# Third pair of row buffers, a narrower memory update, and a new order table in a two-layer attention and Fourier kernel

## The chip, the cores and the metric

The kernel runs on one core of a Trainium2 chip. The metric is the device time of one execution in microseconds (us), taken as the median of several runs. Engines are named as the profile names them: PE multiplies matrices (PEld is its weight load), DVE, ACT and POOL are the vector, scalar and GpSimd engines, and SP issues all DMAs here.

## The reference, cut to what matters

Four sublayers follow each other on x of 2048 rows and 512 columns: attention, Fourier mixing, attention, Fourier mixing. Attention is split into four segments of 512 rows and 32 heads of 16 columns:

```python
for s in range(N):                       # N = 4 segments of L = 512 rows
    logits = einsum("bhqd,bhkd->bhqk", qs, ks) * scale + mask
    a_dot = einsum("bhqk,bhkd->bhqd", softmax(logits), vs)
    pq = phi(qs)                         # phi(t) = t + 1 if t > 0 else exp(t)
    a_mem = einsum("bhld,bhde->bhle", pq, M) / (einsum("bhld,bhd->bhl", pq, z) + 1e-6)
    o = g * a_mem + (1 - g) * a_dot      # outs.append(o)
    M = M + einsum("bhld,bhle->bhde", phi(ks), vs)      # the memory update
    z = z + phi(ks).sum over l
# x = x + A(layernorm(x)); x = x + real(DFT_seq(DFT_hidden(layernorm(x)))), twice
```

The mask hides keys behind the query.

## The kernel before

The heads are worked on in four *groups* of eight heads (`HG = 8`, as two halves `a` of `NP = 4` pairs `p`). A group in a segment of a layer has the number `i` from 0 to 31; `q = i // 4` is its segment over both layers. Its steps are small Python generators ("streams", `s_...`, one for each kind of work, and "tasks", `t_...`, one for each tile). A planner (`Plan`) keeps a modelled clock for each engine. In a loop it takes the step that could start first, less the advance that `LEAN` gives to this kind of step on this engine, and records its instructions. So the code is written out once, in one fixed order for each engine; on the chip, each engine runs its list in that order and waits on semaphores where data is late. `yield need(...)` is a point at which another step may come between.

The path of a group at the start of the program:

- `t_ln` normalizes a tile of 128 rows of x: statistics on DVE (`bst`, `mv`), the power and two small operations on POOL (`rs`), the scaled copy on ACT, its split into two 16-bit halves `hl`. In the first segment (`direct`) PE transposes it with `identh`, and the result goes to the x tile `g` (`xt`). Projections (`s_p`) wait for all four x tiles of the segment.
- `s_w` finds the largest weight (`absmax`, rows named `amax` and `vm`), makes power-of-two scales (`gmax`, `scl`, `inv`, `fac`) and splits the weights (`split`, `share`) that were staged in rows of the result tile `y`. `t_big` later reads `wo` and `wd` into `y`, `s_wo` finds their largest elements (`pmax`) and splits them; its end is the key `WO`, for which the output projection and the Fourier part wait.
- `t_split` turns q and k into halves, stores them to a scratch `d`, and reads them back in rows `qst` and `kst`. There are `NR = 2` pairs of these row buffers; group `i` may write pair `i % 2` only when the scores of group `i - 2` are through (`ST`).
- `s_x` (X) forms the scores `b<-kst,qst` to find each row's largest one. DVE reads them from PSUM and writes `junk` and `mx`; PE transposes `mx` with `identf`, and `mhl` goes into rows of `qst` by DMA. `s_st` (ST) forms them again, transposed (`b<-qst,kst`); ACT takes the exponential, POOL selects. Two rows of ones per half in `kst` (`KR`) are written by `t_ones`.
- `s_av` (AV) multiplies with `vt`: `b<-w,vt`, in which `vt` is the weight operand, 32 columns wide, and four pairs stand side by side in the array. `s_mem` updates the memory: `b<-vt,w`, with `vt` the moving operand; the result is masked with `bd` and added to `macc`. `s_m` merges to `ot`, and `s_o` projects with `b<-wo,w`.

The tile `vt` holds, for each row and pair, 16 columns of one head's v, 16 ones and 16 columns of the other's:

```python
vt = [const.tile([128, TT, NP, 3, 16], F32, name=f"vt{i}") for i in range(NR)]
```

The Fourier part (`b<-wd,w`, then `b<-w,w`) follows, and fills PE wherever attention leaves room. `t_warm` puts idle multiplications (`b<-onesb`) where the planner expects PE to idle, so that PE's clock stays up. Profile rows carry one line number, that of the recording helper (L272), so rows are told apart by tile names.

Of the kernel before, what the change touches and what calls it, by code (L numbers as in the profile page):

```python
# [19 lines left out]
TT = L // 128  # L20
# [11 lines left out]
TICK = 10240 / 3  # L32
LEAN = dict(s_stT=150.0, s_memV=40.0, s_wV=80.0, s_rY=150.0, t_mergeA=40.0, s_xA=150.0, t_abA=40.0, t_mergeY=-150.0, s_mV=40.0, t_cV=-40.0, s_cA=-80.0, s_oY=40.0, t_cY=80.0, t_lnG=80.0, t_splitV=-40.0, t_phiA=150.0, s_kV=-300.0, t_mergeV=150.0, s_cT=80.0, s_avT=80.0, s_wA=-150.0, t_resV=-150.0, t_selG=40.0, s_lnY=-150.0, t_rowsY=300.0, t_ktY=-80.0)
APART = dict(pj=(1, 4), av=(1, 2), dft=(0, 2), sx=(2, 4), st=(2, 4), ss=(0, 4))
# [7 lines left out]
PRIO = {}  # L42
PHM, EARLYLN, FEW = 5, 1, 0
WARM, IDLE, SPARE = 4200, 500.0, 300.0
DEEP = 1500.0
# [4 lines left out]
class Plan:  # L50
# [31 lines left out]
    def key(self, a):  # L82
        f = self.fine.get(a.tensor.name)
        return (a.tensor.name, a.offset // f) if f else a.tensor.name

# [69 lines left out]
    def op(self, eng, name, args, kw):  # L155
# [19 lines left out]
        elif eng == "A":  # L175
            c = n / 1.2 + (52 if src else 93) + (93 if any(a.free_size() == 1 for a in ins) else 0)
        elif eng == "V":
            c = 68 + n / 0.96
            if name == "reciprocal":
                c = 68 + n * 6.25  # L180
            elif name == "scalar_tensor_tensor" and out[0].dtype == F32:
                c += 60
            elif name == "tensor_copy" and out[0].dtype == F16:
                c = 68 + n / 1.92
            elif name == "tensor_scalar" and out[0].dtype == F32:
                c = 68 + n / (0.87 if src else 1.32)
        elif eng == "G":
            c = 127 + n * 0.915 if name == "affine_select" else 96 + n * 2.1
            if name == "tensor_tensor" and kw.get("op") == OP.pow:
                c = 300 + n * 165  # L190
# [88 lines left out]
def body(ctx: ExitStack, tc: tile.TileContext, x, wq, wk, wv, wo, beta, wd, cs, out):  # L279
# [66 lines left out]
    cmask = const.tile([128, 512], BF16, name="cmask")  # L346
    bd = const.tile([128, 2, 4, 32], F32, name="bd")
    gt = const.tile([128, 2, NG, 2], F32, name="gt")
# [64 lines left out]
    def share(o, src, s):  # L413
        yield need("A", src, s)
        A.activation(o[:, 0], src, AF.Copy, scale=s)
        A.activation(src, src, AF.Copy, scale=s)
        yield need("VG", o, src)
        tt(o[:, 1], src, o[:, 0], OP.subtract)

    def flat(t):  # L420
# [104 lines left out]
    def t_ones():  # L525
# [7 lines left out]
        pl.close(c8)  # L533
        for i in range(NR):
            for a in range(2):
                yield need("Y", d8, mode="b")
                Y.dma_start(kst[i][64 * a + 48:64 * a + 50].rearrange("r p n -> r (p n)"), d8, est=(415, 341, 472))
        done.add("KR")

    def s_k():  # L540
# [12 lines left out]
        for j in range(NR):  # L553
            V.memset(vt[j][:, :, :, 1, :], 1.0)
        done.add("VI")
        yield need("V")
        bits(rp, 3, 1.0)
        bits(ra, 64, 1.0 / 64)
        cj = sb("en", F32, (128, 2, 4, 32))
        G.iota(cj, pattern=[[0, 2], [1, 4], [0, 32]], base=0, channel_multiplier=0,  # L560
# [24 lines left out]
    def t_ln(src, xi, dst, key, direct=False):  # L585
        st = rg("bst", 2, F32, (128, 6))
        V.bn_stats(st, src)
        mv = rg("mv", 6, F32, (128, 4))
        V.bn_aggr(mv[:, 0:2], st)
        yield need("G", mv)  # L590
        rs = rg("rs", 6, F32, (128, 1))
        G.tensor_scalar(mv[:, 2:3], mv[:, 1:2], 1e-5, 2.0 ** -20, op0=OP.add, op1=OP.mult)
        G.tensor_tensor(rs, mv[:, 2:3], mhalf, op=OP.pow)
        G.tensor_scalar(mv[:, 3:4], mv[:, 0:1], rs, -1.0, op0=OP.mult, op1=OP.mult)
        yield need("A", src, mv, rs, tag="hl")
        hl = sb("hl", F16, (128, 2, 512))
        A.activation(xi, src, AF.Identity, bias=mv[:, 3:4], scale=rs)
        if direct and pl.free["V"] < pl.free["A"]:
            yield need("V", xi)
            V.tensor_copy(hl[:, 0], xi)  # L600
        else:
            A.activation(hl[:, 0], xi, AF.Copy)
        yield need("VG", xi, hl)
        tt(hl[:, 1], xi, hl[:, 0], OP.subtract)
        pl.close(xi)
        if direct:
# [6 lines left out]
            yield need("VA", p)  # L613
            if pl.free["A"] <= pl.free["V"]:
                A.activation(dst, p, AF.Copy)
            else:
                V.tensor_copy(dst, p)
# [33 lines left out]
    def t_merge(e, o, gi, g, n, key):  # L651
# [7 lines left out]
        rc = rg("rc", 4, F32, (128, 2, 16))  # L659
        xa = x[:, 0]  # L660

        def view(off, *dims):
            return bass.AP(xa.tensor, xa.offset + off, [list(xa.ap[0])] + [list(d) for d in dims])

        yield need("V", x)
        d = view(16, (496, 2), (32, 16))
        if not gi:
            V.tensor_scalar(rc, d, 1e-6, None, op0=OP.add)
            d = rc
        V.reciprocal(rc, d)  # L670
# [3 lines left out]
        for a in range(2):  # L674
            c = slice(16 * a, 16 * a + 16)
            tt(n.rearrange("p (b r) -> p b r", r=32)[:, :, c], view(528 * a, (32, 16), (1, 16)),
               rc[:, a].unsqueeze(2).to_broadcast([128, 16, 16]), OP.mult)
# [3 lines left out]
    def t_split(p, key, f, kphi):  # L681
# [24 lines left out]
        dst = (qst if order else kst)[i % NR]  # L706
        for a in range(2):
# [52 lines left out]
    def t_v(p, i):  # L760
        yield need("A", p)
        A.activation(vt[i % NR].rearrange("p t j e d -> p (t j) e d")[:, :, 0:3:2, :],
                     p.rearrange("p t (j e d) -> p (t j) e d", j=NP, e=2), AF.Copy, scale=2.0 ** -24)
        pl.close(p)
        done.add(("v", i))
# [72 lines left out]
    def s_mem():  # L838
        for i in range(NGRP):
# [14 lines left out]
            if s < NSEG - 1:  # L854
                yield gate(("phk", i), ("v", i), "GM")
                phk, v = phs["phk", i], vt[i % NR]
                yield need("T", phk, v, tag="pj")
                mp = ps("pj", F32, (128, NP, 48))
                for t in range(TT):
                    T.matmul(mp, phk[:, 128 * t:128 * t + 128], v[:, t], start=(t == 0), stop=(t == TT - 1))  # L860
                    yield need("T")
                pl.close(phk)
                yield need("V", mp, tag="mu" if s else ())
                mu = macc[:, g] if s == 0 else sb("mu", F32, (128, 2, 4, 32))
                for a in range(2):
                    V.tensor_tensor(mu[:, a], mp[:, :, 16 * a:16 * a + 32], bd[:, a], op=OP.mult)
                pl.close(mp)
# [16 lines left out]
    def t_max(sp, mx, a, p0, w, t, left):  # L884
        n = 128 * (t + 1)
        for p in range(p0, p0 + w):
            o = (p - p0) * n
            yield need("V", sp)
            junk = rg("junk", 2, BF16)
            V.tensor_tensor_reduce(junk[:, :n], sp[:, o:o + n], cmask[:, 512 - n:], 1.0, -3e38,  # L890
# [4 lines left out]
    def s_x():  # L895
        for i in range(NGRP):
            yield gate(("dq", i), ("dk", i), "CM")
            qs, ks = qst[i % NR], kst[i % NR]
            mx = rg("mx", 2, F32, (128, 2, NP, TT))
# [46 lines left out]
    def s_st():  # L946
        for i in range(NGRP):
            yield gate(("X", i), "KR")
            qs, ks = qst[i % NR], kst[i % NR]
            kt = scores("t")  # L950
# [142 lines left out]
    def t_c(i, raw, sc, cc):  # L1093
        A.activation(cc[:, 0], raw, AF.Copy, scale=sc)
        A.activation(raw, raw, AF.Copy, scale=sc)
        yield need("VG", cc, raw)
# [7 lines left out]
    def s_c():  # L1104
        k = u = 0
        while u < nunit:
# [17 lines left out]
            pl.close(pm)  # L1124
            gi = gv.bitcast(I32)
            V.tensor_scalar(gi, gi, 0x7F800000, None, op0=OP.bitwise_and)
            V.tensor_scalar(csc[:, :m].bitcast(I32), gi, -1.0, float(268 << 23), op0=OP.mult, op1=OP.add)
            V.tensor_scalar(fyu[:, u:u + m], gv, f_y, None, op0=OP.mult)
# [87 lines left out]
    def t_warm(at):  # L1216
        at -= SPARE
        if "CM" not in done or at - pl.free["T"] < IDLE or pl.lately(at) >= WARM:
            return
# [108 lines left out]
```

## Time and profile before

| what | value |
|---|---|
| median of 3 runs | 1696.49 us (1695.97 to 1700.98) |
| the profiled execution, its own time | 1699.92 us |
| its span, first to last instruction | 1698.2 us |
| mean granted clock of PE | 0.989 |
| busy share PE, DVE, ACT, POOL | 98, 61, 51, 48 % |

An engine's "busy" is the time in which at least one of its instructions was under way. Matmuls are pipelined, so their means (380 ns for 512 columns) are longer than the pace at which they follow each other. A row of the groups reads: engine, operation, out<-in, shapes, count, then busy us and mean ns of one, then the idle time before them and who ended it. In the timeline a row gives start, length, and how many equal instructions in a row it stands for. PE writes two instructions for one multiplication of 32-bit operands, so the 96 of the memory update are 192 rows.

### The profile page before, as it was taken

To read this page: it belongs to the slowest core of one execution; us is meant where nothing else is said; L and a number is where in the kernel's file an instruction comes from. 1 tells how busy PE (TensorE), PEld (TensorE's weight loads), DVE (VectorE), ACT (ScalarE), POOL (GpSimd) and SP (SyncE) were. 2 spreads that over 40 slices of the span, in tenths; PEclk is the share of its full clock that TensorE was granted. 3 is DMA by queue.
4 is the path that set the end of the run, shared out by engine and by line. 5 is a ranking of instruction groups with operands and counts; after the bars stand their busy time and mean duration, and the time that the engine had idled before them with its cause. 6 is when DMAs were issued, how large, how long until landed. Compare 5 with 4: busy or idle time off the path is not lost.

```text
span 1698.2 us, 32247 instructions
## 1 busy us (share of the span) xinstructions
PE 1662.3 (98%) x11145; PEld 734.7 (43%) x11145; DVE 1036.8 (61%) x3262; ACT 872.3 (51%) x1480; POOL 810.3 (48%) x1445
## 2 busy tenths in 40 slices
PE   8889999999999999999999999999999999999999
PEld 4344344444444344444544444443444444444444
DVE  8784865778677786635768558546575765433221
ACT  5487577755656666535376754655455325312000
POOL 4376556575565556634255644635454415322000
PEclk9789999999999999999999999999999999999999
DMA  7546545655357432525746663543435322131423
GB/s 182 147 116 178 128 132 159 172 142 152 94 148 208 126 119 84 189 56 196 193 148 187 182 179 90 132 116 98 140 91 149 105 85 76 57 125 38 143 70 123
DMA packets 208629, 222.92 MB, mean 131 GB/s; under 512 B 104520, under 2 KB 127048, under 8 KB 208464
## 3 DMA queue, kind: packets, MB, share of 16 engines
q1 hardware_dynamic: 208464, 220.85, 45.8%
q8 instruction: 88, 1.44, 0.4%
q14 instruction: 77, 0.63, 0.1%
HBM read 137.40 MB, written 61.87 MB: 117 GB/s over the span
## 4 chain that ended last, share of the span: by engine, by line
PE 77%; DVE 9%; ACT 5%; issue 4%; DMA 3%; POOL 2%; SPq 1%; ACTq 0%; DVEq 0%; POOLq 0%
PE b L272 77%; ACT w L272 4%; DVE junk L272 4%; SPq L272 1%; DVE w L272 1%; POOL w L272 1%; DMA w<-w 1%; DMA w<-x 1%; DVE m L272 1%; DVE mx L272 1%; DVE y L272 1%; DVE bst L272 0%; DVE cam L272 0%; DMA w<-in_cs_dram 0%; DVE pmax L272 0%
## 5 line engine op out<-in xcount | busy, mean ns | idle before, releaser
L272 PEld LDWEIGHTS <-w 128*128 128x128 f16 x5056 | 467.8, 98 | 612.8 <-issue 101.1
L272 PE MATMUL b<-w,w 128*128 128x512 f16 x3072 | 708.5, 380 | 1.7 <-DVE mx L272 0.8
L272 ACT ACTIVATE w<-b,fac 128x512 f32<-128x512 f32 (+1 forms) x728 | 419.2, 655 | 176.3 <-PE b L272 175.8
L272 DVE CUSTOM_DVE_ANT_0 junk<-b,cmask 128x128 bf16<-128x128 f32 (+3 forms) x1024 | 436.3, 483 | 71.6 <-PE b L272 71.1
L272 POOL TENSOR_TENSOR w<-w,w 128x512 f16<-128x512 f32 (+1 forms) x294 | 347.5, 1187 | 247.1 <-ACT w L272 223.6
L272 POOL TENSOR_SCALAR_AFFINE_SELECT w<-w 128x128 f32<-128x128 f32 (+2 forms) x704 | 237.0, 350 | 202.7 <-ACT w L272 194.1
L272 DVE SCALAR_TENSOR_TENSOR y<-b,fyu,y 128x512 f32<-128x512 f32 x200 | 148.9, 745 | 235.6 <-PE b L272 235.2
L272 ACT ACTIVATE w<-w,csc 128x512 f16<-128x512 f32 (+1 forms) x256 | 180.1, 720 | 41.5 <-DVE csc L272 32.8
L272 PE MATMUL b<-g,w 128*128 128x512 f16 x768 | 183.1, 383 | 3.2 <-DMA g<-w 0.8
L272 PE MATMUL b<-wd,w 128*128 128x512 f16 x768 | 176.8, 379 | 0.1
L272 PE MATMUL b<-w,vt 128*32 128x512 f32 (+3 forms) x2048 | 172.4, 449 | 1.9 <-POOL w L272 1.1
L272 ACT ACTIVATE w<-b 128x512 f16<-128x512 f32 x128 | 75.9, 596 | 189.4 <-PE b L272 179.3
L272 DVE SCALAR_TENSOR_TENSOR w<-b,w 128x512 f16<-128x512 f32 x128 | 87.6, 687 | 120.3 <-ACT w L272 118.7
L272 ACT ACTIVATE w<-w 128x512 f16<-128x512 f32 (+1 forms) x137 | 86.5, 632 | 90.1 <-DVE w L272 87.9
L272 PE MATMUL b<-kst,qst 48*128 48x128 f16 (+3 forms) x1024 | 117.5, 304 | 6.3 <-DVE mx L272 3.2
L272 PE MATMUL b<-qst,kst 50*128 50x512 f16 (+3 forms) x1024 | 115.8, 302 | 5.5 <-DVE mx L272 2.2
L272 PE MATMUL b<-w,g 128*128 128x128 f16 x1536 | 96.3, 221 | 0.0
L272 PEld LDWEIGHTS <-g 128*128 128x128 f16 x1536 | 89.6, 99 | 12.7 <-issue 7.8
L272 DVE STREAM_TRANSPOSE m<-b 128x512 f32<-128x512 f32 x112 | 75.6, 698 | 31.1 <-PE b L272 30.7
L272 PEld LDWEIGHTS b<-w,vt 128*32 128x32 f32 x2048 | 54.8, 110 | 87.7 <-issue 48.2
L272 PE MATMUL b<-wo,w 128*128 128x512 f16 x384 | 89.1, 379 | 0.0
L272 PEld LDWEIGHTS <-kst 50*128 50x128 f16 x1024 | 37.3, 94 | 111.7 <-issue 105.2
(105 smaller groups left out, 1019.3 us busy)
## 6 DMA issues: line engine op xcount, KB each, us to landing
w<-in_cs_dram SPq DMA_DIRECT2D x128, 256.0 KB, 3.5
cc<-w SPq DMA_DIRECT2D x128, 256.0 KB, 3.2
w<-cc SPq DMA_DIRECT2D x128, 256.0 KB, 3.1
w<-w SPq DMA_DIRECT2D x96, 256.0 KB, 3.5
d<-w SPq DMA_DIRECT2D x128, 128.0 KB, 2.5
w<-in_x_dram SPq DMA_DIRECT2D x32, 256.0 KB, 3.6
qst<-d SPq DMA_DIRECT2D x64, 128.0 KB, 2.7
kst<-d SPq DMA_DIRECT2D x64, 128.0 KB, 3.3
```

The costliest lines, as they stand in the source:

```text
L272: r = f(*args, **kw)
```

## The change

1. A third pair of row buffers lies in rows 8 to 11 of the result tile `y`, where the value weights were staged. It serves group 2 alone, once all value weights are split. Groups 3 and on use pairs 0 and 1 in turn (`ring`) and wait for the group named in `prior`: group 3 for ST of group 0 (before: of group 1), group 4 for ST of group 1 (before: of group 2), and from group 5 on as before.
2. `vt` is `[128, TT, 32, HG]`: 16 rows of v columns, then 16 of ones, the eight heads innermost. The update reads the first 17 of the 32 (136 columns, before 192); AV takes 32 columns that lie 8 elements apart (before: side by side). The mask is applied in two pieces of the same number of elements, and `bd` is 16 bits wide. The value weights are permuted on the host to fit.
3. In the first segment the small operations of the norms run on DVE, except the power, and the split of the x tile always on DVE.
4. More `yield need(...)` stand between instructions of one tile. The making of `bd` waits for the first scales.
5. Some costs of the planner and some entries of `LEAN` are new, and warming may start before the causal mask is made.

```diff
-LEAN = dict(..., t_abA=40.0, ..., s_oY=40.0, ..., s_cT=80.0, ...)
+LEAN = dict(..., t_abA=150.0, ..., s_cT=150.0, ..., s_ldY=300.0, t_lnA=80.0, t_lnY=-150.0)
...
+    kst.append(y[:, 8:10, :].bitcast(F16).rearrange("p a (b n) -> p (a b) n", n=512))
+    qst.append(y[:, 10:12, :].bitcast(F16).rearrange("p a (b n) -> p (a b) n", n=512))
+    ring = [0, 1, 2] + [(i - 3) % 2 for i in range(3, NGRP)]
+    prior = [None] * 3 + [0, 1] + list(range(3, NGRP - 2))
-    vt = [const.tile([128, TT, NP, 3, 16], F32, name=f"vt{i}") for i in range(NR)]
+    vt = [const.tile([128, TT, 32, HG], F32, name=f"vt{i}") for i in range(NR)]
...
+        if direct and STARTV:
+            yield need("V", mv)
+            V.tensor_scalar(mv[:, 2:3], mv[:, 1:2], 1e-5, 2.0 ** -20, op0=OP.add, op1=OP.mult)
+            yield need("G", mv)
+            G.tensor_tensor(rs, mv[:, 2:3], mhalf, op=OP.pow)
+            yield need("V", mv, rs)
+            V.tensor_scalar(mv[:, 3:4], mv[:, 0:1], rs, -1.0, op0=OP.mult, op1=OP.mult)
...
-        if i >= NR:
-            yield gate(("ST", i - NR))
+        if i == NR:
+            yield gate(*[("W", 2, g) for g in range(NG)])
+        elif i > NR:
+            yield gate(("ST", prior[i]))
...
-                mp = ps("pj", F32, (128, NP, 48))
+                mp = ps("pj", F32, (128, 17, HG))
-                    T.matmul(mp, phk[:, 128 * t:128 * t + 128], v[:, t], start=(t == 0), stop=(t == TT - 1))
+                    T.matmul(mp, phk[:, 128 * t:128 * t + 128], v[:, t, :17], start=(t == 0), stop=(t == TT - 1))
...
-                                 v[:, t, p].rearrange("k e d -> k (e d)")[:, 16 * a:16 * a + 32], tiles[p][1],
+                                 v[:, t, :, NP * a + p], tiles[p][1],
```

How this moves instructions is seen at two places. The first is DVE at the start, up to the copy of the fourth x tile. Before, the statistics of all four tiles stand together ahead of the weights' scales (the rows begin behind the statistics of the first two tiles; `w_85` to `w_91` are the four tiles of x, `w_319` and `w_329` their halves):

```order
L272 BN_STATS bst<-w_89 128x6
L272 BN_AGGR mv<-bst 128x2
L272 BN_STATS bst<-w_91 128x6
L272 BN_AGGR mv<-bst 128x2
L272 CAST w_319<-w_85 128x512
L272 CAST w_329<-w_87 128x512
L272 TENSOR_REDUCE amax<-y 128x1 x2
L272 TENSOR_SCALAR gmax<-b_365 128x2
```

Now the last part of the fourth tile (`w_91`, its halves `w_450`) stands among the scales of the last weights:

```order
L279 CAST w_450<-w_91 128x512
L279 TENSOR_SCALAR gmax<-b_471 128x2
L279 TENSOR_SCALAR gmax<-gmax 128x2
L279 TENSOR_SCALAR scl<-gmax 128x2
L279 TENSOR_SCALAR inv<-gmax 128x2
L279 TENSOR_SCALAR fac<-inv 128x1 x4
L279 TENSOR_REDUCE amax<-y 128x1 x2
L279 TENSOR_TENSOR w_450<-w_91,w_450 128x512
```

Eight small scale instructions behind these rows comes DVE's copy of the fourth tile to the x tile `g`. From the first statistics to it DVE now has 76 instructions. Before, its one copy to `g` was the 18th, and the other three tiles' copies were ACT's.

The second place is SP's queue between the scores X of groups 1 and 2. Before, the row maxima `mhl` of group 1 go out first, then the stores `d` of groups 2 and 3, and the rows of group 2 (into pair 0, `qst_106`) after them:

```order
L272 DMA qst_107<-mhl 1x16x128 x4
L272 DMA d<-w_810 64x2x512 x2
L272 DMA d<-w_1209 64x2x512 x2
L272 DMA_TRANSPOSE w_1239<-w_1209 128x8x128
L272 DMA w_1261<-in_x_dram 128x512
L272 DMA d<-w_1241 64x2x512 x2
L272 DMA d<-w_1268 64x2x512 x2
L272 DMA qst_106<-d 32x2048
```

Now the rows of group 2 go into `y` right behind the row maxima of group 1, and those of group 3 into pair 0 behind them:

```order
L279 DMA d<-w_834 64x2x512 x2
L279 DMA d<-w_1196 64x2x512 x2
L279 DMA d<-w_1252 64x2x512 x2
L279 DMA qst_107<-mhl 1x16x128 x4
L279 DMA y<-d 32x2048
L279 DMA y<-d 16x2048
L279 DMA y<-d 32x2048
L279 DMA y<-d 16x2048 x2
L279 DMA y<-d 32x2048
L279 DMA y<-d 16x2048
L279 DMA y<-d 32x2048
L279 DMA qst_106<-d 32x2048
```

The rows of group 2 no longer wait for the scores of group 0, but they still stand behind `mhl` of group 1.

More of the change, by code (lines that the diff above doesn't have):

```diff
@@ L418, in share, with view @@
         tt(o[:, 1], src, o[:, 0], OP.subtract)
+    def view(t, off, *dims):
+        return bass.AP(t.tensor, t.offset + off, [list(t.ap[0])] + [list(d) for d in dims])
     def flat(t):
@@ L659, in t_merge @@
         rc = rg("rc", 4, F32, (128, 2, 16))
[L660 to L663 removed]
         yield need("V", x)
[L666 removed]
+        d = view(x, 16, (512, 2), (32, 16))
         if not gi:
             V.tensor_scalar(rc, d, 1e-6, None, op0=OP.add)
+            if YM:
+                yield need("V", rc)
             d = rc
@@ L701, in t_split @@
             spawn(t_kt(hl, kphi))
-        if i >= NR:
-            yield gate(("ST", i - NR))
+        if i == NR:
+            yield gate(*[("W", 2, g) for g in range(NG)])
+        elif i > NR:
+            yield gate(("ST", prior[i]))
         yield need("Y", d)
         order = key[0] == "dq"
-        dst = (qst if order else kst)[i % NR]
+        dst = (qst if order else kst)[ring[i]]
         for a in range(2):
@@ L897, in s_x @@
             yield gate(("dq", i), ("dk", i), "CM")
-            qs, ks = qst[i % NR], kst[i % NR]
+            qs, ks = qst[ring[i]], kst[ring[i]]
             mx = rg("mx", 2, F32, (128, 2, NP, TT))
@@ L947, in s_st @@
         for i in range(NGRP):
-            yield gate(("X", i), "KR")
-            qs, ks = qst[i % NR], kst[i % NR]
+            yield gate(("X", i), ("KR", ring[i]))
+            qs, ks = qst[ring[i]], kst[ring[i]]
             kt = scores("t")
@@ L1217, in t_warm @@
         at -= SPARE
-        if "CM" not in done or at - pl.free["T"] < IDLE or pl.lately(at) >= WARM:
+        if at - pl.free["T"] < IDLE or pl.lately(at) >= WARM:
             return
```

74 lines of the change are left out of this document (53 added, 21 removed).

## The prediction, as put on record

> **What bounds the kernel now.** The page comes first: is one engine the bound, and where is it not?
>
> ```profile
> span 1698.2 us, 32247 instructions
> PE 1662.3 (98%) x11145; PEld 734.7 (43%) x11145; DVE 1036.8 (61%) x3262; ACT 872.3 (51%) x1480; POOL 810.3 (48%) x1445
> PE   8889999999999999999999999999999999999999
> PEclk9789999999999999999999999999999999999999
> PE 77%; DVE 9%; ACT 5%; issue 4%; DMA 3%; POOL 2%; SPq 1%; ACTq 0%; DVEq 0%; POOLq 0%
> ```
>
> PE is busy in all slices but the first three or four, and carries 77% of the chain that ended last. So work that is taken from PE behind the start comes off the end, and in the start it is the other engines that decide. The second view is the table of stretches, cut at the events that the timeline shows:
>
> ```profile
> core 0: us, PE busy (x) PEld busy (x) DVE busy (x) ACT busy (x) POOL busy (x), PEclk, DMA share, GB/s
> 0.00:17.00 17.00, 11.34 (x62) 5.11 (x63) 14.10 (x40) 9.35 (x11) 10.07 (x25) 1.00 0.96 247
> 34.00:70.00 36.00, 30.71 (x156) 10.23 (x154) 34.36 (x144) 15.08 (x25) 10.42 (x18) 0.83 0.60 177
> 70.00:91.00 21.00, 20.65 (x175) 10.10 (x174) 8.88 (x30) 14.73 (x27) 12.78 (x25) 0.89 0.62 129
> 91.00:132.00 41.00, 35.55 (x258) 14.68 (x255) 33.59 (x146) 33.98 (x61) 30.15 (x59) 0.79 0.36 96
> 132.00:172.00 40.00, 38.80 (x352) 18.00 (x349) 20.68 (x69) 29.77 (x52) 27.65 (x50) 1.00 0.65 189
> 213.00:1698.00 1485.00, 1469.24 (x9796) 650.20 (x9796) 875.02 (x2675) 733.17 (x1244) 689.09 (x1226) 1.00 0.45 129
> ```
>
> Up to 172 us PE does few instructions per us (156 in 36 us, against 9796 in 1485), partly at a reduced clock (0.79 to 0.89). DVE fills 34 to 70 (34.36 of 36 us), where X of groups 0 and 1 runs, and is nearly idle from 70 to 91. The third view is PE's timeline, for the dates:
>
> ```profile
> 16.88 1.46 PE L272 MATMUL b<-g,w 128*128 128x512 f16 x6 [0.68 <-ACT g L272]
> 18.31 4.04 PE L272 MATMUL b<-g,w 128*128 128x512 f16 x18
> 34.39 0.51 PE L272 MATMUL b<-kst,qst 48*128 48x128 f16 x10
> 69.74 0.39 PE L272 MATMUL b<-identf,mx 128*32 128x128 f32 x1 [1.56 <-DVE mx L272]
> 90.67 0.42 PE L272 MATMUL b<-kst,qst 48*128 48x128 f16 x8
> 131.24 0.27 PE L272 MATMUL b<-identf,mx 128*32 128x128 f32 x1 [0.94 <-ACT w L272]
> 171.61 0.60 PE L272 MATMUL b<-wo,w 128*128 128x512 f16 x2
> ```
>
> The first projections, q and k of group 0, run from 16.88 to 22.35; X of groups 0 and 1 from 34.39 to 69.74 (`identf` is its end); X of group 2 starts at 90.67, and that of group 3 ends at 131.24; the first output projection, from which PE has enough to do, is at 171.61. The hole from 69.74 to 90.67 is the wait for a free pair of row buffers.
>
> **The memory update.** 96 multiplications stand as 192 instructions:
>
> ```profile
> L272 PE MATMUL b<-vt,w 128*128 128x192 f32 x192 | 38.6, 338 | 1.4 <-ACT vt L272 1.2 <-POOL w L272 0.2
> L272 PE MATMUL b<-vt,w x192: 326/326/430, 79.6 to 1260.2; 128*128 128x192 f32 x192
> 79.55 1.57 PE L272 MATMUL b<-vt,w 128*128 128x192 f32 x8
> 82.16 0.92 PE L272 MATMUL b<-vt,w 128*128 128x192 f32 x4
> ```
>
> Four more instructions in a row cost 1.57 - 0.92 = 0.65 us, so the pace is 162.5 ns for 192 columns, 0.846 ns a column. With 136 it is 115 ns if only the columns count: 47 ns saved. What could hold it up is the weight load of 128 columns that lies beside each. The first of a run, whose load has no cover, takes 430 ns against 326, so a load costs 104 ns: just under 115. I take the full 47 ns; the other bound is nothing saved, if a load of 32-bit weights needs more than its 104 ns beside a running matmul. In both orders 20 of the 96 stand ahead of the first output projection, where PE waits anyway; the other 76 are 152 instructions x 47 ns = **-7.1 us** (bounds -7.1 and 0). DVE's mask has as many elements as before, now with a step between them in PSUM; DVE idles for 610 of 1485 us behind 213 and covers it; without that cover it would be 96 pieces with, at most, 0.2 us more each.
>
> **The weight operand of AV**, with a step of 8 elements. Its loads stand beside each other and beside a running matmul:
>
> ```profile
> L272 PEld LDWEIGHTS b<-w,vt 128*32 128x32 f32 x2048 | 54.8, 110 | 87.7 <-issue 48.2 <-POOL w L272 23.4 <-DVE mx L272 3.0
> 81.05 0.85 PE L272 MATMUL b<-w,vt 128*32 128x384 f32 x8
> 81.84 0.39 PE L272 MATMUL b<-qst,kst 50*128 50x256 f16 x4
> ```
>
> At 0.846 ns a column, four side by side, a load of 110 ns lies beside matmuls of 108 ns (128 columns) to 433 ns (512); only the first load behind another kind of work lies open, about 120 times by the order. Of its 110 ns the reading of 32 columns is some 26, a quarter of the 104 of 128 columns. No row shows a stepped load. Bounds: 0 (the same elements; nothing can be gained), and the whole 110 ns once more each time, 13 us. I take 0: most of a load is not reading.
>
> The Trainium skill ("Advanced Engine Details and Errata", SBUF Cachelines) speaks against the change: a line is 16 bytes, full speed needs at least two hits on each, and here neighbours are 32 bytes apart. By that rule, as an estimate at half speed, reading takes 26 ns more at each open load: 3.1 us, and 1691 for the whole. No run here shows it yet; the mechanism is in the third rival.
>
> **Changes of PE's kind of work.** From AV to scores above, 81.84 - 81.05 = 0.79 us, of which 8 x 384 columns, four side by side at 0.846 ns, are 0.65: 0.14 us a change. Behind the first Fourier product the order has 726 such changes before and 749 now: 23 x 0.14 = **+3.2 us**.
>
> **The start.** The 76 instructions that DVE now has ahead of the fourth x tile, by these rows:
>
> ```profile
> 4.24 0.68 DVE L272 BATCH_NORM_STATS2 bst<-w 128x6 f32<-128x512 f32 x1
> 8.60 0.45 DVE L272 CAST w<-w 128x512 f16<-128x512 f32 x1 [0.51 <-ACT w L272]
> 14.28 0.69 DVE L272 COPY g<-b 128x1024 f16<-128x1024 f16 x1 [0.21 <-PE b L272]
> 14.89 1.63 DVE L272 SCALAR_TENSOR_TENSOR w<-y,scl,w 128x512 f16<-128x512 f32 x2
> 19.30 0.17 DVE L272 TENSOR_SCALAR scl<-gmax 128x2 int32<-128x2 int32 x1
> 19.57 0.40 DVE L272 TENSOR_SCALAR fac<-inv 128x1 f32<-128x1 f32 x4
> 19.89 2.46 DVE L272 TENSOR_REDUCE vm<-y 128x1 f32<-128x512 f32 x4
> 25.16 0.68 DVE L272 SCALAR_TENSOR_TENSOR w<-b,w 128x512 f16<-128x512 f32 x1
> L272 DVE TENSOR_TENSOR wd<-y,wd 128x512 f16<-128x512 f32 x1 | 0.9, 912 | 5.4 <-ACT y L272 5.4
> ```
>
> Four each of statistics (0.68), casts (0.45) and subtractions (0.91): 8.2 us; 12 reductions at 0.615: 7.4; four aggregates, 20 scale and 8 norm instructions and a last small reduction at 0.17: 5.6; 16 `fac`: 1.6; two copies and two weight splits: 3.0. Sum 25.8. It starts at about 4, so the first projection comes at about **30 against 16.88**. Before, the split of group 0's k came on DVE at 25.16, 2.8 us behind its projection, since weight reductions stood ahead; now these are done, and I give 2 us of it back. So X of group 0 starts 15.5 instead of 17.5 us behind the first projection, at 45.5 (34.39). X of groups 0 and 1 is DVE's 34.4 us, and ends at 79.9 (69.74). Now the third pair counts. The rows of group 2 stand on SP behind the last store of group 3 and the row maxima:
>
> ```profile
> 79.76 3.05 SPq L272 DMA_DIRECT2D d<-w  x4
> 70.46 2.41 SPq L272 DMA_DIRECT2D qst<-mhl  x4
> 83.43 1.74 SPq L272 DMA_DIRECT2D qst<-d  x4
> kst<-d SPq DMA_DIRECT2D x64, 128.0 KB, 3.3
> ```
>
> 1.5 us for two stores (3.05 for four), 2.4 for the maxima, 3.5 for eight issues of rows (1.74 for four), 3.3 to land: 10.7, so X of group 2 starts at **90.6 against 90.67**. The hole shrinks from 20.9 to 10.7 us, and the late first projection eats it. From there to the end of X of group 3 it was 40.6 us, with DVE busy for 33.6 of 41. Group 3's rows now wait only for ST of group 0 and come early; between these two ends I take 37.4: end at 128.0 (131.24). What is late next is AV and the merge of group 3, with `WO` (40.4 us, ACT busy for 29.8 of 40), taken as before. First output projection at 168.4: **-3.2 us**. By the order 22 more score matmuls stand ahead of it, which PE needn't do later: two side by side, some 320 columns, against 1.46 / 6 = 0.24 us for 512, make 0.075 each, **-1.6 us**.
>
> More idle matmuls (111, before 83) fill time in which PE waits in the start; at 0.22 us each they cost 6 us if PE were not waiting there, and I count none, since DVE's 25.8 us cover them. The other yields cost nothing by themselves: they are the order.
>
> **Sum.** -7.1 + 3.2 - 3.2 - 1.6 = -8.7 us. Against the profiled execution's own 1699.92 that is 1691.2, 0.5% less. That execution is 3.4 us above the median of the runs, so for the median 1696.49 - 8.7 = **1687.8**, said as 1688.
>
> **Rivals.**
>
> *The late first projection stays (slower).* The hole is perhaps not the buffer's alone: in 70:91 PE is busy for 20.65 of 21 us, with scores, AV, update and projections that have to be done in any case. If that work, and not the rows, sets when X of group 2 starts, the hole stays at 20.9 us, and the 13 us by which the first projection is late reach the first output projection: 13 - 7.1 + 3.2 - 1.6 = +7.5, **1704**. For it: the clock of 0.89 there. Against: X stands in the order by its data, and its matmuls are a fraction of a us each. Slower begins at 10.6 us of lateness left at the first output projection.
>
> *The start shortens in full.* If X of groups 2 and 3 runs at DVE's pace (33.6) and the merge of group 3 follows 6 us sooner since its scores no longer wait, the first output projection comes 3.8 + 6 us sooner than I say: **1678**. For it: 20.9 us of hole, and clocks of 0.79 and 0.89 that denser work would lift. Against: ACT is busy for 34 of 41 us in 91:132 too.
>
> *The loads cost.* Either AV's stepped loads lie open for half of 110 ns more (120 x 55 = +6.6), or the update saves nothing (+7.1): about **1694**, no measurable change. For it: 104 ns of load under 115 of matmul is a thin cover. Against: today's pace is set by the columns, and a load of AV is a quarter reading.
>
> **How the numbers follow.** The forecast has a chance of 0.50 (own range 1682 to 1694), the full start 0.18, the costly loads 0.17, the late start 0.15. This kernel's runs tell a change of 0.3%, 5.1 us: below 1691.4 is faster, above 1701.6 slower. Of the forecast 0.43 lies below; with the full start's 0.18 and a little of the loads (0.04), faster is 0.65. Slower is most of the late start, 0.13; the same is the rest, 0.22. The range from 1676 to 1702 leaves out half of the late start and a third of the full one, under 2 in 10.
>
> **What would show it.** The update's 192 instructions with 136 columns at a pace near 115 ns, runs of eight near 1.2 us. AV's loads still at 110 ns, and eight of them with 384 columns in 0.85 us. The first projection near 30 us, X of group 2 near 90, the first output projection near 168. If the first projection comes at 20 or X of group 2 before 80, the start gains more than I say; if the first output projection comes behind 180, the change loses.

## The result and the profile after

The changed kernel takes 1832.6 us (median of 4 runs, 1827.3 to 1837.9) against 1698.7 for the kernel before on the same chip: a ratio of 1.079, 95% interval 1.075 to 1.083. It is 8% slower, where 0.5% faster was forecast. The page after, its first lines and the line of the chain:

```profile
span 1831.2 us, 32352 instructions
PE 1717.9 (94%) x11173; PEld 752.0 (41%) x11173; DVE 1108.5 (61%) x3294; ACT 868.9 (47%) x1478; POOL 794.1 (43%) x1415
PE 65%; DVE 22%; issue 5%; DMA 3%; ACT 3%; SPq 2%; POOL 1%; DVEq 0%; ACTq 0%; POOLq 0%
```

DVE carries 22% of the chain that ended last, 9% before, and is busy for 72 us more, though it has only 32 more instructions. The table of stretches after, with the cuts of the prediction:

```profile
core 0: us, PE busy (x) PEld busy (x) DVE busy (x) ACT busy (x) POOL busy (x), PEclk, DMA share, GB/s
34.00:70.00 36.00, 33.10 (x220) 15.25 (x217) 21.07 (x76) 8.43 (x16) 4.57 (x4) 0.85 0.71 183
91.00:132.00 41.00, 36.85 (x329) 18.27 (x328) 26.51 (x99) 27.19 (x49) 23.28 (x47) 0.82 0.58 143
132.00:172.00 40.00, 27.32 (x142) 9.04 (x139) 25.10 (x90) 25.14 (x45) 22.14 (x40) 0.66 0.30 80
213.00:1831.00 1618.00, 1544.98 (x9971) 676.07 (x9968) 957.37 (x2768) 754.38 (x1283) 699.63 (x1245) 0.99 0.44 121
```

The loss has two parts. From 132 to 172 us PE did 352 instructions before and does 142 now, so the start is worse. And PE is no longer always busy behind 213: 73 of 1618 us are open, where 16 of 1485 were. PE's timeline gives the dates:

```profile
30.94 7.03 PE L279 MATMUL b<-g,w 128*128 128x512 f16 x24 [2.31 <-DVE bits L279]
95.63 0.39 PE L279 MATMUL b<-identf,mx 128*32 128x128 f32 x1 [0.59 <-DVE mx L279]
111.04 0.39 PE L279 MATMUL b<-y 48*128 48x128 f16 x8
164.66 0.28 PE L279 MATMUL b<-identf,mx 128*32 128x128 f32 x1
211.15 2.75 PE L279 MATMUL b<-wo,w 128*128 128x512 f16 x12 [0.26 <-ACT vt L279]
```

The rows are the first projection, the end of X of group 1, the start of X of group 2 (its rows lie in `y`), the end of X of group 3, and the first output projection. That last one comes at 211.15 instead of 171.61, 39.5 us late; from it to the end of the span there are 1620.1 us instead of 1526.6, 93.5 more.

What DVE does differently is seen in its timeline, in a run of row maxima of 384 columns, before and then after. Only the maxima are shown; behind each stands a read of 0.08 us that puts the maximum into `mx`:

```profile
58.05 0.55 DVE L272 CUSTOM_DVE_ANT_0 junk<-b,cmask 128x384 bf16<-128x384 f32 x1
58.52 0.55 DVE L272 CUSTOM_DVE_ANT_0 junk<-b,cmask 128x384 bf16<-128x384 f32 x1
59.00 0.55 DVE L272 CUSTOM_DVE_ANT_0 junk<-b,cmask 128x384 bf16<-128x384 f32 x1
```

```profile
57.30 0.56 DVE L279 CUSTOM_DVE_ANT_0 junk<-b,cmask 128x384 bf16<-128x384 f32 x1
58.01 0.56 DVE L279 CUSTOM_DVE_ANT_0 junk<-b,cmask 128x384 bf16<-128x384 f32 x1
58.72 0.56 DVE L279 CUSTOM_DVE_ANT_0 junk<-b,cmask 128x384 bf16<-128x384 f32 x1
```

One instruction takes as long as before (0.55 and 0.56 us). But before, the next began every 0.475 us, while the last was still under way; now it begins every 0.71 us, 0.15 us behind the other's end. The cause is one line of the change that neither its description nor the prediction mentions:

```diff
-            junk = rg("junk", 2, BF16)
+            junk = rg("junk", 1, BF16)
```

`junk` is the tile into which a row maximum writes the elements that nobody reads. With one such tile every maximum writes over the tile of the one ahead of it, and waits for that write; with two, it is the one before that, long done. There are 1024 maxima, 256 of each width. In the same stretches the pace grew by 0.235 us at 384 and 512 columns, by 0.17 at 256 and 0.14 at 128. If every maximum stood directly behind another, that would make 256 x 0.78 = 200 us more of DVE's time; in the changed kernel 831 of the 1024 are directly followed by another. What it came to is seen in the rows of the whole group, before and after:

```profile
L272 DVE CUSTOM_DVE_ANT_0 junk<-b,cmask 128x128 bf16<-128x128 f32 (+3 forms) x1024 | 436.3, 483 | 71.6 <-PE b L272 71.1
L279 DVE CUSTOM_DVE_ANT_0 junk<-b,cmask 128x128 bf16<-128x128 f32 (+3 forms) x1024 | 500.0, 488 | 146.9 <-PE b L279 62.0
```

The busy time grew by 64 us, and the idle time before the maxima that PE did not end grew from 0.5 to 84.9 us. Together that is about 150 us.

### The profile page after: what moved, and what is told of

Its sections match the earlier page's. It is cut to its first block, busy times and chain, and to the rows that moved or that the text cites. A ratio compares the mean times of both kernels' runs of the same rounds, so it can differ in the third digit from the quotient of the medians.

```text
span 1831.2 us, 32352 instructions
## 1 busy us (share of the span) xinstructions
PE 1717.9 (94%) x11173; PEld 752.0 (41%) x11173; DVE 1108.5 (61%) x3294; ACT 868.9 (47%) x1478; POOL 794.1 (43%) x1415
## 4 chain that ended last, share of the span: by engine, by line
PE 65%; DVE 22%; issue 5%; DMA 3%; ACT 3%; SPq 2%; POOL 1%; DVEq 0%; ACTq 0%; POOLq 0%
PE b L279 65%; DVE junk L279 16%; ACT w L279 2%; DMA w<-w 2%; SPq L279 2%; DVE w L279 1%; DVE y L279 1%; DVE mx L279 1%; DVE cam L279 1%; DVE m L279 1%; POOL w L279 0%; DMA w<-in_x_dram 0%; DVE bst L279 0%; DMA g<-w 0%; DVEq L279 0%
## 5 line engine op out<-in xcount | busy, mean ns | idle before, releaser
L279 DVE CUSTOM_DVE_ANT_0 junk<-b,cmask 128x128 bf16<-128x128 f32 (+3 forms) x1024 | 500.0, 488 | 146.9 <-PE b L279 62.0
L279 ACT ACTIVATE w<-b,fac 128x512 f32<-128x512 f32 (+1 forms) x728 | 424.1, 653 | 223.0 <-PE b L279 221.1
L279 POOL TENSOR_TENSOR w<-w,w 128x512 f16<-128x512 f32 (+1 forms) x283 | 334.5, 1190 | 214.7 <-ACT w L279 187.5
L279 ACT ACTIVATE w<-w,csc 128x512 f16<-128x512 f32 (+1 forms) x256 | 175.1, 721 | 27.5 <-DVE csc L279 19.6
L279 PE MATMUL b<-qst,kst 50*128 50x512 f16 (+1 forms) x992 | 128.2, 304 | 33.7 <-DVE mx L279 30.0
L279 PE MATMUL b<-kst,qst 48*128 48x128 f16 (+1 forms) x992 | 129.1, 308 | 20.6 <-DVE mx L279 17.1
L279 PEld LDWEIGHTS b<-w,vt 128*32 128x32 f32 x2048 | 67.8, 145 | 83.7 <-issue 48.2
L279 DVE STREAM_TRANSPOSE m<-b 128x512 f32<-128x512 f32 x112 | 75.0, 696 | 38.9 <-PE b L279 34.6
## 6 DMA issues: line engine op xcount, KB each, us to landing
d<-w SPq DMA_DIRECT2D x128, 128.0 KB, 2.5
qst<-d SPq DMA_DIRECT2D x62, 128.0 KB, 3.0
```

Source lines behind the costliest of these rows:

```text
L279: r = f(*args, **kw)
```

## The experiments

The theory at this point, J: the single `junk` tile makes almost all of the loss. The rival, O: the loss is the order, with its late first projection, and the tile only fills waiting time. (The expectations call it S; their L is that AV's stepped loads make the loss.) Two kernels try the tile alone, on both sides; a third has the update and the stepped loads alone; a fourth takes the third pair of row buffers away.

**e1: the changed kernel with two junk tiles.** Room for it comes from laying three small constants into parts of `macc` that are not yet used, and from two `rc` buffers instead of four; what these moves do is in e1's time too, while e2 has none of them. The order of all engines is that of the changed kernel.

```diff
-            junk = rg("junk", 1, BF16)
+            junk = rg("junk", 2, BF16)
```

> The changed kernel with two buffers for the row-maximum's scratch output (junk) instead of one; the kilobyte for it comes from small tiles laid into macc and from two rc buffers instead of four. All five engines keep the changed kernel's order. Theory J (one junk buffer: each of the 1024 maxima on DVE waits until the one before has written): the pace of a 512-column maximum goes from 844 ns back to about 613, about 230 ns less on each of 1024, and the time falls by 120 to 145 us, to 1688 to 1710. Rival L (AV's stepped weight loads, 139 ns against 110, cost the time): stays above 1810. Rival S (the new order with its late first projection costs it): falls by under 40 us, above 1790.

Measured: 1714.1 us (1712.6 to 1716.7), ratio to the kernel before 1.011 (1.009 to 1.013), where the changed kernel has 1.079: 115 us less by the ratios, 118 by the medians. That is just under the 120 to 145 of the expectation.

**e2: the kernel before with one junk tile**, and nothing else changed.

```diff
-            junk = rg("junk", 2, BF16)
+            junk = rg("junk", 1, BF16)
```

> The kernel before with one junk buffer instead of two and nothing else; same order on all engines. J: slower by 110 to 145 us, 1810 to 1845, with 512-column maxima 844 ns apart. L and S: within 20 us of the kernel before, since DVE idles for 39% of the span and would cover it.

Measured: 1816.8 us (1811.4 to 1817.9), ratio 1.071 (1.068 to 1.073), 121 us more. The same run of maxima, in e1 and then in e2:

```profile
55.14 0.55 DVE L279 CUSTOM_DVE_ANT_0 junk<-b,cmask 128x384 bf16<-128x384 f32 x1
55.62 0.55 DVE L279 CUSTOM_DVE_ANT_0 junk<-b,cmask 128x384 bf16<-128x384 f32 x1
```

```profile
67.44 0.56 DVE L272 CUSTOM_DVE_ANT_0 junk<-b,cmask 128x384 bf16<-128x384 f32 x1
68.15 0.56 DVE L272 CUSTOM_DVE_ANT_0 junk<-b,cmask 128x384 bf16<-128x384 f32 x1
```

The pace goes with the number of tiles, 0.48 and 0.71, whatever kernel it stands in, and the time goes with the pace. J is shown, in sign and size; O falls as the main cause, and so does L, since e1 keeps the stepped loads. Of about 150 us of DVE time 115 to 121 reach the end.

**e3: the kernel before with the new layout of `vt`**: update by 136 columns and stepped loads, in the old order (two junk tiles as it has them, constants laid into `macc` and two `rc` buffers as in e1, the mask in two pieces and `bd` in 16 bits). The line of AV:

```diff
-                                 v[:, t, p].rearrange("k e d -> k (e d)")[:, 16 * a:16 * a + 32], tiles[p][1],
+                                 v[:, t, :, NP * a + p], tiles[p][1],
```

> The kernel before with the new layout of vt alone: update of 136 columns, mask in two pieces, AV's loads with a step of 8 elements, two junk buffers. The planner is made to count the old sizes, so all engines keep the order of the kernel before. J: the update saves 47 ns on 192 instructions, 7 to 9 us where PE is the bound, and the stepped loads give back 29 ns at some 120 open places, 3.5 us: 1692 to 1697. L: slower than before by over 50 us.

Measured: 1695.1 us (1692.2 to 1699.2), ratio 0.9994 (0.9981 to 1.0007): no change that can be told.

**e4: e1 without the third pair of row buffers**, planned anew.

```diff
-    ring = [0, 1, 2] + [(i - 3) % 2 for i in range(3, NGRP)]
+    ring = [i % 2 for i in range(NGRP)]
```

> The changed kernel with two junk buffers as in the first run of this call, and without the third pair of row buffers: group 2 waits for the scores of group 0 again. The planner makes a new order. J with the third pair filling the hole of the start as predicted: 8 to 12 us slower than the first run, since X of group 2 starts some 10 us later behind the late first projection. Rival (the hole is filled by other work in any case): within 4 us of the first run.

Measured: 1728.3 us (1727.4 to 1733.0), ratio 1.020 (1.017 to 1.022): 14 us over e1, more than the 8 to 12 that were expected. Taken alone, this says that the third pair is worth 14 us. e8 will show that it isn't.

What was open now is e1's own 18 us over the kernel before. PE's timeline of e1 shows where it loses:

```profile
31.22 6.93 PE L279 MATMUL b<-g,w 128*128 128x512 f16 x24 [2.11 <-DVE bits L279]
85.58 0.40 PE L279 MATMUL b<-identf,mx 128*32 128x128 f32 x1
100.90 0.39 PE L279 MATMUL b<-y 48*128 48x128 f16 x8
129.96 0.58 PE L279 MATMUL b<-y 50*128 50x512 f16 x1 [4.97 <-DMA y<-mhl]
131.61 1.48 PE L279 MATMUL b<-kst,qst 48*128 48x128 f16 x12
147.65 0.28 PE L279 MATMUL b<-identf,mx 128*32 128x128 f32 x1
192.06 2.76 PE L279 MATMUL b<-wo,w 128*128 128x512 f16 x12
```

The first output projection comes 20.45 us later than before (171.61), and from there to the end it is 1519.7 us, 6.9 less than before. So all of the rest is lost in the start. Part of it can be named. Before, X of group 3 stood ahead of ST of group 2 on PE, and began right behind X of group 2:

```profile
112.56 0.27 PE L272 MATMUL b<-identf,mx 128*32 128x128 f32 x1
113.44 0.61 PE L272 MATMUL b<-kst,qst 48*128 48x128 f16 x12
117.78 0.69 PE L272 MATMUL b<-qst,kst 50*128 50x512 f16 x4
```

Now ST of group 2 (`50*128`, rows in `y`) stands ahead, and PE waits 4.97 us for its row maxima `mhl`, while X of group 3, at 131.61, queues behind it.

**e5: a pure delay at the start.** e3 in its own order, with idle fills ahead of a copy to `g`.

```diff
             else:
+                for _ in range(52):
+                    nc.vector.memset(macc[:, 1], 0.0)
                 V.tensor_copy(dst, p)
```

> The kernel of e3 (before, with the 136-column update and the stepped loads; 1695.1 us) in its own order, but with 52 fills of 256 columns of an unused part of macc put on DVE ahead of its copy of an x tile to g. Before's fills of vt take 0.27 us each, so DVE, and with it the first projection, comes 14 us later; nothing else is changed. Theory S (what is lost at the start reaches the end, since PE has no slack behind 213 us): 12 to 15 us more, 1707 to 1710. Rival A (the start has a hole of some 20 us from 70 to 91 us that takes it up): 0 to 5 us more, 1695 to 1700.

Measured: 1737.9 us (1735.9 to 1740.2), 42.8 over e3. This is three times what was expected, for two reasons that the trace shows. The rows are e3's first projection, then e5's fills on DVE, its first projection, and PE's wait at the start of the second attention sublayer:

```profile
17.65 1.46 PE L275 MATMUL b<-g,w 128*128 128x512 f16 x6 [0.68 <-ACT g L275]
14.83 20.25 DVE L624 MEMSET macc<- 128x256 f32 x52
35.77 2.72 PE L275 MATMUL b<-g,w 128*128 128x512 f16 x6 [17.76 <-DVE g L275]
839.81 4.46 PE L275 MATMUL b<-g,w 128*128 128x512 f16 x14 [20.79 <-DVE g L275]
```

The fills all write the same tile, and they follow each other every 0.39 us; the two fills of `vt` in the kernel before, into two tiles, follow each other after 0.27. This fits the same wait as that of `junk`. And this branch is passed twice, once in each attention sublayer. So PE was held up by 18.1 us (35.77 against 17.65) and by 20.8, together 38.9, and the end came 42.8 us later. The two can be told apart at the first output projection, which comes at 189.72 in e5 and at 168.79 in e3: the 18.1 us of the start are 20.9 there. Read that way, S holds: a delay of DVE's whole start reaches the end in full, and A falls.

**e6: e3 with the update widened back to 192 columns**, so that of the new layout the stepped loads are left, with the two-piece mask and the moved constants and buffers.

```diff
-                    T.matmul(mp, phk[:, 128 * t:128 * t + 128], v[:, t, :17], start=(t == 0), stop=(t == TT - 1))
+                    T.matmul(mp, phk[:, 128 * t:128 * t + 128], v[:, t, :24], start=(t == 0), stop=(t == TT - 1))
```

> The kernel of e3 with the update widened again to 192 columns, so that only the stepped weight loads of AV are left of the new layout of vt. Theory U (the narrower update is worth its 152 x 47 ns = 7 us, and e3 showed no gain since the stepped loads cost about as much): 6 to 7 us over e3, 1701 to 1702, and so 5 to 6 us over before. Rival W (neither reaches the end: both lie under other work): 1695 to 1697, like e3 and before.

Measured: 1700.0 us (1697.1 to 1702.7, 12 runs), ratio 1.0022 (1.0014 to 1.0031): 3.7 us over the kernel before, and 4.9 us over e3. So the narrower update is worth some 5 us, less than the 6 to 7 of U, and the rest of the layout costs about as much. That this rest is the loads is not shown by e6 alone: the buffers moved too. The mask is not it, since a piece of it into `macc` takes 282 ns in the median in the kernel before and in e3.

**e7 to e10: orders that fit.** In e1 and e4 a table `LEAN` is used that was given with the changed kernel. So e7 is e1 with another table, e8 is e4 with another, e9 is e1 with the first norms as before, and e10 is e3 with the third pair; each has a table of its own, found in the same way by the planner's model alone. For e9 and e10 the core of the edit, cut (`STARTV` at 0 sends the small operations of the norms back to POOL, `YB` at 0 takes out the `yield` behind the statistics):

```diff
-STARTV, YL, YB, YM, YC, YS = 1, 1, 1, 1, 1, 1
+STARTV, YL, YB, YM, YC, YS = 0, 1, 0, 1, 1, 1
...
-        if direct:
-            yield need("V", xi, hl)
-            V.tensor_tensor(hl[:, 1], xi, hl[:, 0], op=OP.subtract)
-        else:
-            yield need("VG", xi, hl)
-            tt(hl[:, 1], xi, hl[:, 0], OP.subtract)
+        yield need("VG", xi, hl)
+        tt(hl[:, 1], xi, hl[:, 0], OP.subtract)
```

```diff
+    kst.append(y[:, 8:10, :].bitcast(F16).rearrange("p a (b n) -> p (a b) n", n=512))
+    qst.append(y[:, 10:12, :].bitcast(F16).rearrange("p a (b n) -> p (a b) n", n=512))
+    ring = [0, 1, 2] + [(i - 3) % 2 for i in range(3, NGRP)]
```

> The kernel of e1 (after with two junk buffers, 1714.1 us) with another table LEAN: the best of some 530 randomly changed tables by the modelled clocks of the kernel's own planner (no time is taken from these). It gives e1 the same chance as the three kernels beside it, which got tables in the same way. Theory N (the rest of the loss is the late first projection, which the norm steps on DVE make): the first projection stays near 31 us, and the time near e1's, 1706 to 1714. Theory T (the loss is an order that fits badly, of any cause): below 1704.

> The kernel of e4 (as e1, but without the third pair of row buffers; 1728.3 us) with a table of its own, found as for e7 in some 450 tries. Theory P (the third pair is worth the 14 us by which e4 stood over e1): 10 us or more over e7. Rival T (e4 ran with a table that had been made for another set of steps, and lost by the order): 0 to 5 us over e7.

> The kernel of e7 with the first norms as before: scale operations on POOL, no step behind the statistics, the split of an x tile on POOL or DVE. All else is as in after with two junk buffers, third pair included; a table of its own in 450 tries. Theory N (norm steps on DVE make the first projection late, and that reaches the end): first projection near 20 us or sooner, and 8 to 14 us less than e7. Rival T: the same as e7 within 4 us.

> The kernel of e3 (before's start, two junk buffers, 136 columns) plus the third pair of row buffers, with a table of its own in 450 tries. Theory N and the third pair together: first projection near 17 to 20 us, X of group 2 sooner, 1680 to 1690, less than before. Rival T (the order decides, and start and pair don't): within 4 us of e7.

| kernel | us (range) | ratio to before (interval) | first projection |
|---|---|---|---|
| e7, all of the change, two junk tiles | 1699.0 (1695.4 to 1703.3) | 1.0019 (1.0007 to 1.0031) | 16.75 |
| e8, without the third pair | 1701.4 (1697.9 to 1703.6) | 1.0028 (1.0013 to 1.0043) | 31.05 |
| e9, first norms as before | 1692.6 (1689.2 to 1694.4) | 0.9978 (0.9968 to 0.9987) | 17.39 |
| e10, before's start and third pair | 1689.5 (1687.9 to 1692.9) | 0.9962 (0.9947 to 0.9977) | 17.95 |

The first projections in PE's timelines of e7 and e8:

```profile
16.75 1.46 PE L279 MATMUL b<-g,w 128*128 128x512 f16 x6 [0.90 <-ACT g L279]
31.05 5.34 PE L279 MATMUL b<-g,w 128*128 128x512 f16 x24 [2.47 <-DVE bits L279]
```

By the table alone, e7 is 15 us under e1, and its first projection comes at 16.75 with the norms still on DVE. So N, as it was put, falls: the norm steps don't make the first projection late, the order does. T holds for 15 of e1's 18 us. Nor is a late first projection alone decisive: e8 has it at 31.05 and is only 2.3 us over e7. e5 doesn't contradict this, since there everything on DVE came late, while in e8 DVE prepares weights in that time which are then done: X of group 1 ends at 87.40 in e8 and at 89.45 in e7. P falls too: with tables of their own, e8 is 2.3 us over e7, with intervals that overlap, and not 14. e9 is 6.5 us under e7, less than the 8 to 14 of N and more than the 4 of T. How much of this is the norms is not shown, since each kernel has one table of its own, and a table alone moved e1 by 15 us and e4 by 27. e10 is as expected, below the kernel before.

The date of the first output projection is no measure across tables. In e10 it comes at 179.33, 7.7 us later than in the kernel before, but from there to the end of the span it is 1508.8 us, 17.8 less.

**e11: e10 without the third pair**, with its own table, and **e12: e10 with `vt` laid out as before**, in e10's order; the update's 136 columns are then eight pieces of 17. The line of the update:

```diff
-                    T.matmul(mp, phk[:, 128 * t:128 * t + 128], v[:, t, :17], start=(t == 0), stop=(t == TT - 1))
+                    T.matmul(mp, phk[:, 128 * t:128 * t + 128], view(v, 192 * t, (48, NP), (31, 2), (1, 17)), start=(t == 0), stop=(t == TT - 1))
```

> The kernel of e10 without the third pair of row buffers (so: before's steps, two junk buffers, 136 columns, stepped loads), with a table of its own in some 450 tries. Theory P2 (the third pair still helps where the first projection is early): 3 to 6 us over e10, 1692 to 1696. Rival T (only the table was gained in e10): within 2 us of e10, 1688 to 1691.5.

> The kernel of e10 in the same order, but with vt laid out as before (16 columns of one head, 16 ones, 16 columns of the other), so that AV's weight loads take 32 neighbouring columns again; the update still reads 136 columns, 17 at a time (31 elements between the starts). Theory L (the step of 32 bytes makes AV's loads slower, 139 instead of 110 ns, and this reaches the end): loads back at 110 ns, update pace still near 116 ns, 3 to 4 us under e10, 1685 to 1687. Rival: the loads are hidden and e6's 3.5 us came from elsewhere: the same as e10 within 1.5 us; or the broken rows of 17 slow the update: 2 to 5 us over e10.

Measured: e11 1689.1 us (1687.7 to 1690.4), ratio 0.9965 (0.9953 to 0.9977); e12 1689.8 us (1686.1 to 1692.5), ratio 0.9971 (0.9959 to 0.9982). Both are as fast as e10. So the third pair brings nothing that can be told even beside an early start, and P2 falls. e11 has the steps of e3, so its table alone makes 5 us by the ratios. L, in e12, is not borne out: its loads are short again (below), yet no gain shows. e10, e11 and e12 beat both kernels, by 0.3 to 0.4% against the kernel before.

## Why the prediction was wrong

**The step that failed first: the list of what changes.** The sum has terms for update, loads, changes of kind, start and score matmuls. It has no term for `junk`. Its own words on DVE, that it "idles for 610 of 1485 us behind 213 and covers it", would have given 0 for it too: 150 to 200 us of more DVE time against 610 idle. e1 and e2 show it at 115 and 121 us. Idle time on average doesn't cover it, because the scores of a group and its maxima are one chain, in which PE waits for DVE. Ahead of PE's score matmuls, the idle time that a maximum (`mx`) ended was 3.2 and 2.2 us before, and is 17.1 and 30.0 us now:

```profile
L272 PE MATMUL b<-kst,qst 48*128 48x128 f16 (+3 forms) x1024 | 117.5, 304 | 6.3 <-DVE mx L272 3.2
L272 PE MATMUL b<-qst,kst 50*128 50x512 f16 (+3 forms) x1024 | 115.8, 302 | 5.5 <-DVE mx L272 2.2
L279 PE MATMUL b<-kst,qst 48*128 48x128 f16 (+1 forms) x992 | 129.1, 308 | 20.6 <-DVE mx L279 17.1
L279 PE MATMUL b<-qst,kst 50*128 50x512 f16 (+1 forms) x992 | 128.2, 304 | 33.7 <-DVE mx L279 30.0
```

The chain that ended last, by line, has the maxima at 4% before and at 16% after:

```profile
PE b L272 77%; ACT w L272 4%; DVE junk L272 4%; SPq L272 1%; DVE w L272 1%; POOL w L272 1%; DMA w<-w 1%; DMA w<-x 1%; DVE m L272 1%; DVE mx L272 1%; DVE y L272 1%; DVE bst L272 0%; DVE cam L272 0%; DMA w<-in_cs_dram 0%; DVE pmax L272 0%
PE b L279 65%; DVE junk L279 16%; ACT w L279 2%; DMA w<-w 2%; SPq L279 2%; DVE w L279 1%; DVE y L279 1%; DVE mx L279 1%; DVE cam L279 1%; DVE m L279 1%; POOL w L279 0%; DMA w<-in_x_dram 0%; DVE bst L279 0%; DMA g<-w 0%; DVEq L279 0%
```

The planner could not see it either: its model (`Plan.op`) skips the wait for a tile's last write where DVE itself wrote it last and the next operation has "reduce" in its name, as `tensor_tensor_reduce` has.

A page's rule could have misled as well. The Trainium skill ("VectorE: DVE Perf Modes", The DRAIN you can't avoid) says that DVE's next operation cannot issue until the pipe of the last is empty, and that in its measurement of eight copies a semaphore behind each cost nothing extra; it adds that a next operation which is not held starts earlier. The trace agrees with the addition, and for these instructions not with the rest: with two tiles the next one starts 0.475 us behind a start of 0.55 us length, and the wait on the tile costs 0.235 us at this width.

**The start, -3.2 us.** The first projection near 30 was right (30.94), but what follows was not. In e1, without the junk wait, X of group 1 ends at 85.58 (forecast 79.9), X of group 2 starts at 100.90 (90.6), X of group 3 ends at 147.65 (128.0), and the first output projection is at 192.06 (168.4). The term is +20.45 instead of -3.2, and the 23.65 us between them lie in four steps. The way to the end of X of group 1 took 5.7 us more than the sum gave it. The step "the hole shrinks from 20.9 to 10.7 us, and the late first projection eats it" left 15.3 us of hole, 4.6 more. The 37.4 us from there to the end of X of group 3 were 46.75, 4.97 of them the new wait for `mhl`. And the 40.4 us from there to the first output projection were 44.4. The rival of the late start, with 0.15, had the outcome, lateness that reaches the first output projection, but by a hole that stays at 20.9; its 1704 is 10 under e1. e7 adds that the lateness belongs to the table more than to the norms, and e11 against e10 that no gain of the third pair can be told.

**The update, -7.1 us.** The pace is as forecast. Rows of the changed kernel, the timeline's runs of four and eight, and e12's run of eight in pieces of 17:

```profile
134.07 0.73 PE L279 MATMUL b<-vt,w 128*128 128x136 f32 x4 [0.69 <-ACT vt L279]
189.91 1.19 PE L279 MATMUL b<-vt,w 128*128 128x136 f32 x8
187.54 1.25 PE L276 MATMUL b<-vt,w 128*128 128x136 f32 x8
```

Four more instructions cost 0.46 us, so 115 ns each. What reaches the end is somewhat less, though the forecast 7.1 lies just within the noise: the ratios of e6 and e3 differ by 0.0028, 4.7 us, give or take 2.6. The mask's 0.2 us a piece, which the prediction gives as a bound, is not seen in any run: a piece into `macc` takes 282 ns in the median before and 283 in the changed kernel.

**The loads, 0.** The reading under it, that a stepped load takes no longer, is wrong. In all kernels with the new layout a load takes 138 to 139 ns in the median (the changed kernel first), and in e12, laid out as before, 109:

```profile
L279 PEld LDWEIGHTS b<-w,vt x2048: 135/139/178, 85.6 to 1628.9; 128*32 128x32 f32 x187
L276 PEld LDWEIGHTS b<-w,vt x2048: 106/109/178, 66.2 to 1458.1; 128*32 128x32 f32 x187
```

That is some 29 ns more, near the 26 that the prediction had beside its 0. By that rule (the Trainium skill, "Advanced Engine Details and Errata", SBUF Cachelines) elements on a line each are slow; the trace agrees. Whether it reaches the end stays open: e6 gives 3.7 us (2.4 to 5.3) for the loads and the moved buffers together, while e12 shows no gain over e10, with intervals of 2 to 2.5 us each and a slower update against it.

**Changes of kind, +3.2, and score matmuls, -1.6.** They were not tried by themselves. Together with the update they were to make the part behind the first output projection 5.5 us shorter; in e1 it is 6.9 shorter, with the loads in it.

In sum, by the ratios to the kernel before, of the 134 us by which the changed kernel is slower 115 are the junk tile (to e1), 15 the table (to e7), and 3 are left. These 3 are not the price of the other steps, since the kernel before gained by a new table too: with tables of their own on both sides, e7 is 9 us over e11, and up to 6.5 of them may be the norms on DVE (e9).

## What to carry to other kernels

Read the diff for every buffer count and put a price on each, even where the tile's contents are never read: a scratch tile that is written again by the next instruction is a wait. When a part is taken out of a kernel whose order was searched for, search the order anew for both sides before the part gets a price; without that, the third pair seemed worth 14 us, and with it 2.3, with intervals that overlap. An engine's idle share covers added work only where the bounding engine doesn't wait for that very chain.

## What the runs showed of the hardware

DVE's instructions overlap their neighbours when nothing holds them: a maximum of 0.55 us is followed by the next after 0.475. When each writes the tile that the one just ahead has written, the pace is 0.71, and with fills of one tile it is 0.39 us, against 0.27 into two tiles. A weight load of 32 columns of 32-bit elements, 32 bytes apart, takes 138 to 139 ns and not 109 to 110. A moving operand of 136 columns in pieces of 17 elements, whose starts lie 31 and 17 elements apart in turn, costs 123 ns and not 116 in the median (e12, and the changed kernel).
